# A top-1 mixture of experts on one core: the count of left-over tokens in eight portions over the third expert, its registers loaded and a GpSimd DRAIN placed earlier

## The chip, the cores and the metric

One Trainium2 chip, one of its cores. The metric is the device time of one execution in microseconds, lower is better. Engines are named as in the profile: PE is TensorE, DVE is VectorE, ACT is ScalarE, POOL is GpSimd, SP is SyncE, PEld the weight loads of TensorE. A name with a q behind it (POOLq) is the engine's sequencer, the queue that hands instructions to it.

## The reference, cut to what matters

```python
def _attn_ref(q, k, v):                       # 8 batches, 8 heads, 576 positions, 64 wide
    scores = np.matmul(q, k.transpose(0, 1, 3, 2)) / np.sqrt(64)
    return np.matmul(scores * Dmat[None], v)  # Dmat: a decay per head, causal
def _moe_ref(x, w_skip, w_gate, w1, w2):      # x: 4608 tokens x 512; 8 experts, 1024 hidden
    do_compute = x @ w_skip > 0
    out = x.copy()
    xc = x[do_compute]
    e_idx = np.argmax(xc @ w_gate, axis=1)
    gate_w = softmax(xc @ w_gate)[np.arange(len(xc)), e_idx]
    for e in range(8):
        mask = e_idx == e
        y[mask] = gate_w[mask, None] * (np.maximum(xc[mask] @ w1[e], 0.0) @ w2[e])
    out[do_compute] = xc + y
    return out
```

## The kernel before, in words

The first part, up to about 165 us, computes the retention for 36 tiles of 128 tokens, writes the tiles to `out`, and finds for each token its expert, its gate and its rank among the tokens of that expert.

The second part (`experts`, L1104) takes the experts one after the other, in an order found at run time from the largest to the smallest. Each expert has a fixed capacity (`CAPS`: 368, 344, 332, 308, 304, 286, 278, 276). Its tokens are gathered from `out` with three indirect DMAs on GpSimd (`gather_next`, L1059), turned, and split in a high and a low part (`xhi`, `xlo`). There are eight chunks of the hidden size. For a chunk, the up products write `ph`, ScalarE makes `hhi` from it and VectorE `hlo` (`rectify`, L521), and the down products read both and add to `py`. TensorE takes the up products of a chunk ahead of the down products of the chunk before it. After the eighth chunk `py` goes to `yT`, is turned back to token rows (`yn`), VectorE multiplies by the gate and adds the token (`rs`, L1040), and GpSimd scatters the rows to `out` with three indirect DMAs (`put_rows`, L1043). These scatters stand in the next expert, except for those of the first and the last expert. Weights come by SP in chunks of 512 KB; ScalarE makes `whi_w` and VectorE `wlo_w` (L164, L165), about five chunks ahead.

Tokens above a capacity are left over. `count_more` (L952) finds how many blocks of 128 of them there are: a small matmul `pn`, then VectorE instructions for `over`, `big`, `ends`, `sh`, the number `nmore`, and a new rank `trank` for the left-over tokens. It is called once, after the down products issued in chunk five of the last expert:

```python
        at(NE - 1, 4, 1, count_more)
...
    nblock = nc.values_load(nmore[0:1, 0:1], min_val=0, max_val=MAXB + NE)
    with tc.For_i(0, nblock, 1):
```

`at(e, f, place, do)` queues work into expert `e` (from 0), chunk `f` (from 0): place 0 ahead of the down products issued in that chunk, place 1 behind them. `values_load` (L1240) loads the number into a register of each of the five engines. The loop on it (L1241) does the left-over blocks; for these inputs it runs no time, and the kernel goes to its closing barrier (L1339).

TensorE's order is the order of the code (`manual_schedule`). On the other engines a scheduler sets it, guided by `keep_in_program_order`; `vec` (L176) is a VectorE instruction marked so, while `nc.vector...` alone is not. Where an instruction stands is therefore read from the built program, below.

Of the kernel before, what the change touches and what calls it, by code (L numbers as in the profile page):

```python
# [17 lines left out]
ALU = mybir.AluOpType  # L18
AX = mybir.AxisListType
# [3 lines left out]
NTOK, DM, NE, DF = B * S, H * D, 8, 1024  # L23
P = 128
# [5 lines left out]
NFC = DF // P  # L30
# [6 lines left out]
MAXB = -(-NTOK // P)  # L37
# [4 lines left out]
FAR = 1.0e5  # L42
# [23 lines left out]
def kernel(  # L66
# [9 lines left out]
    nc = tc.nc  # L76
# [10 lines left out]
    def bank(tag, name):  # L87

        if tag == "ph":
            tag = f"sc{turn[0] % 2}"  # L90
            turn[0] += 1
        return pm.tile([P, 512], F32, tag=TAGS.get(tag, tag), name=name)
# [16 lines left out]
    trank = const.tile([P, NT], F32, tag="trank", name="trank")  # L109
# [28 lines left out]
    mks = const.tile([P, NT, NE], BF16, tag="mks", name="mks")  # L138
    perm = const.tile([P, NE, NE], F32, tag="perm", name="perm")
    bump = const.tile([P, NE], BF16, tag="bump", name="bump")  # L140
    cape = const.tile([P, NE], F32, tag="cape", name="cape")
# [34 lines left out]
    def vec(name, *args, **kw):  # L176
        ins = getattr(nc.vector, name)(*args, **kw)  # L177
        if pinned[0]:
            tc.keep_in_program_order(ins)
        return ins  # L180
# [309 lines left out]
    nmore = const.tile([P, 1], I32, tag="nmore", name="nmore")  # L490
# [63 lines left out]
    with ExitStack() as actx:  # L554
# [224 lines left out]
        def logits_b(b, lt):  # L779
            pn = bank("lg", f"pn_{b}").rearrange("p (t i) -> p t i", i=P)  # L780
            for o in range(NB):
                nc.tensor.transpose(pn[:, o, :], lt[:, o * P : (o + 1) * P], ident)
            return pn
# [93 lines left out]
        for g in range(NT):  # L877
# [13 lines left out]
            if pn is not None:  # L891
                closed(g // NB - 1, pn)
                pn = None
# [12 lines left out]
            if lt is not None:  # L906
                pn = logits_b(g // NB - 1, lt)
# [19 lines left out]
        pn = logits_b(NT // NB - 1, lt)  # L927
# [18 lines left out]
    xr, xq, xts = {}, {}, {}  # L946

    xg0.append(mp.tile([P, DM], F32, tag="xg0_2", name="xg0_2", bufs=1))
    ends = rt.tile([P, NE], F32, tag="ends", name="ends")
    block = rt.tile([P, 1], F32, tag="block", name="block")  # L950

    def count_more():  # L952

        pn = bank("m", "pn")[:, :NE]
        nc.tensor.matmul(pn, ones, cum[:, len(GROUPS), :], start=True, stop=True)
        over = rt.tile([P, NE], F32, tag="over", name="over")
        nc.vector.tensor_tensor(over, pn, bump, ALU.add)
        nc.vector.tensor_tensor(over, over, cape, ALU.subtract)
        kb = [P, NE, MAXB]
        step = mp.tile([P, MAXB], F32, tag="step", name="step", bufs=1)  # L960
        nc.gpsimd.iota(step, pattern=[[P, MAXB]], base=0, channel_multiplier=0, allow_small_or_imprecise_dtypes=True)
        big = mp.tile(kb, F32, tag="big", name="big", bufs=1)
        nc.vector.tensor_tensor(
            big, over.unsqueeze(2).broadcast_to(kb), step.unsqueeze(1).broadcast_to(kb), ALU.is_gt
        )
        nc.vector.tensor_reduce(ends, big, axis=AX.X, op=ALU.add)

        sh = rt.tile([P, NE], F32, tag="sh", name="sh")
        nc.vector.memset(sh[:, 0:1], 0.0)
        for e in range(1, NE):  # L970
            nc.vector.tensor_copy(sh[:, e : e + 1], ends[:, e - 1 : e])
            nc.vector.tensor_tensor(ends[:, e : e + 1], ends[:, e : e + 1], ends[:, e - 1 : e], ALU.add)
        nc.vector.scalar_tensor_tensor(sh, sh, float(P), cape, ALU.mult, ALU.subtract)
        nc.vector.tensor_copy(nmore, ends[:, NE - 1 : NE])
        nc.vector.memset(block, 0.0)
        cb = [P, NT, NE]
        ct = mp.tile(cb, F32, tag="ct", name="ct", bufs=1)
        sums = []
        for n, x in (("cs", sh), ("cl", cape)):
            nc.vector.tensor_tensor(ct, mks, x.unsqueeze(1).broadcast_to(cb), ALU.mult)  # L980
            sums.append(mp.tile([P, NT], F32, tag=n, name=n, bufs=1))
            nc.vector.tensor_reduce(sums[-1], ct, axis=AX.X, op=ALU.add)
        cs, cl = sums
        nc.vector.tensor_tensor(cl, trank, cl, ALU.is_lt)
        nc.vector.tensor_tensor(trank, trank, cs, ALU.add)
        nc.vector.scalar_tensor_tensor(trank, cl, -FAR, trank, ALU.mult, ALU.add)

    def gather(e, xg, ks):
        for k, n in ks:
# [114 lines left out]
    def experts():  # L1104
# [20 lines left out]
        def at(e, f, place, do, *args):  # L1125
            between.setdefault((e, f, place), []).append(lambda: do(*args))
# [13 lines left out]
        def turn_next(e):  # L1140
# [3 lines left out]
            for c, where in enumerate([(4, 0), (5, 0), (5, 1), (6, 0), (7, 0)]):  # L1144
                if c:
                    at(e - 1, *where, split_turned, e, *xT[e], c - 1)
                if c < NCC:
                    at(e - 1, *where, turn_quarters, e, c)

        at(NE - 1, 4, 1, count_more)  # L1150
        for e in range(2, NE):
            at(e - 2, 4 if e > 2 else NCUT, 1, lambda e=e: gather_next(e, xg))

# [16 lines left out]
        for cur in steps + [None]:  # L1170
            if cur:
                e, f, ks = cur
# [15 lines left out]
            if last:  # L1188
                e, f, ks = last
# [44 lines left out]
    rectify(phs[5], early, hs[0, 5])  # L1234

    experts()
    mctx.__exit__(None, None, None)


    nblock = nc.values_load(nmore[0:1, 0:1], min_val=0, max_val=MAXB + NE)  # L1240
    with tc.For_i(0, nblock, 1):  # L1241
        puts.clear()
        mine = rt.tile([P, NE], F32, tag="mine", name="mine")
# [101 lines left out]
```

## Time and profile before

| | us |
|---|---|
| median of 3 runs | 412.4 (414.35, 406.65, 412.4) |
| the profiled execution | 408.29 |
| its span, first to last instruction | 406.6 |
| TensorE busy | 382.8 (94%) |
| VectorE busy | 260.3 (64%) |
| ScalarE busy | 150.5 (37%) |
| GpSimd busy | 126.5 (31%) |
| the last expert's chunks on TensorE | about 367 to 394 |
| the last row of any compute engine ends | 399.2 |

The span is 1.7 us shorter than the execution's own time. In the timeline a row is the start, the duration, the engine, the line, the operation, its output and inputs, and in brackets how long the engine was idle before it and who ended that. Matmuls overlap: the step from one start to the next is what one costs.

### The profile page before, as it was taken

The page shows a single profiled execution, that of the slowest core. Times are in us where ns is not written, and L with a number is a line of the kernel's source. Part 1 is how long each engine was busy: PE and PEld are TensorE (multiplying, and loading weights), DVE is VectorE, ACT ScalarE, POOL GpSimd, SP SyncE. Part 2 cuts the span into 40 slices and gives each one's busy share as a digit, 9 for nine tenths or more (in the row PEclk, how much of TensorE's full clock was granted, in tenths as well). Part 3 has the DMA queues.
Part 4 walks back from the last instruction along what each step waited for, and adds up shares of the span by engine and source line. Part 5 has one row for each costly group of instructions (what it writes and reads, how often), then busy time and mean ns, then how long its engine had stood idle before and what let it go on. Part 6 is the DMA issues. An engine that isn't in the chain of part 4 may idle for free. (4 is left out here: it accounts for less than half of the span.)

```text
span 406.6 us, 11777 instructions
## 1 busy us (share of the span) xinstructions
PE 382.8 (94%) x4840; PEld 346.4 (85%) x4840; DVE 260.3 (64%) x568; ACT 150.5 (37%) x264; POOL 126.5 (31%) x167
## 2 busy tenths in 40 slices
PE   8989999998999999999999999999999999999970
PEld 4768878777677778888999999999999999999970
DVE  3656775694496946758738566658567767677740
ACT  1222322332333345135435435526536355354110
POOL 5523232242363584260420032133230430402102
PEclk9999999999999999999999999999999999999995
DMA  8999998999999553083896596696786788844001
GB/s 302 408 394 312 389 374 261 358 332 379 389 340 374 188 182 106 24 282 119 266 272 220 194 278 196 200 273 205 214 292 204 228 273 248 254 150 131 23 2 55
DMA packets 38600, 98.50 MB, mean 242 GB/s; under 512 B 4523, under 2 KB 12075, under 8 KB 38544
## 3 DMA queue, kind: packets, MB, share of 16 engines
q1 hardware_dynamic: 29584, 78.13, 57.6%
q0 software_dynamic: 3488, 10.03, 7.3%
q10 hardware_dynamic: 5472, 9.56, 6.3%
q8 instruction: 39, 0.64, 0.7%
q14 instruction: 17, 0.14, 0.1%
HBM read 79.72 MB, written 18.35 MB: 241 GB/s over the span
## 5 line engine op out<-in xcount | busy, mean ns | idle before, releaser
L164 ACT CAST whi_w<-w 128x1024 fp32r<-128x1024 f32 x58 | 60.9, 1051 | 47.9 <-DMA w<-w 25.1
L1044 POOL DMA_INDIRECT out<-rs,sidx x24 | 34.1, 1422 | 135.1 <-DVE rs L1040 134.1
L165 DVE TENSOR_TENSOR wlo_w<-w,whi_w 128x1024 fp32r<-128x1024 f32 x58 | 69.8, 1204 | 0.0
L503 PE MATMUL py<-hlo,whi_w 128*128 128x344 f32 (+6 forms) x224 | 67.9, 303 | 1.7 <-DVE hlo L527 1.6
L503 PE MATMUL ph<-xhi,whi_w 128*128 128x344 f32 (+6 forms) x224 | 68.8, 307 | 0.0
L503 PE MATMUL py<-hhi,whi_w 128*128 128x344 f32 (+6 forms) x224 | 68.2, 305 | 0.0
L503 PE MATMUL ph<-xlo,whi_w 128*128 128x344 f32 (+6 forms) x224 | 67.7, 302 | 0.3 <-DVE xlo L172 0.3
L503 PE MATMUL py<-hhi,wlo_w 128*128 128x344 f32 (+6 forms) x224 | 67.7, 302 | 0.0
L503 PE MATMUL ph<-xhi,wlo_w 128*128 128x344 f32 (+6 forms) x224 | 67.7, 302 | 0.0
L671 POOL TENSOR_TENSOR v<-v,tt_sb 128x512 f32<-128x512 f32 x36 | 37.5, 1043 | 82.7 <-DVE xt L177 59.3
L527 DVE SCALAR_TENSOR_TENSOR hlo<-ph,hhi 128x344 fp32r<-128x344 f32 (+7 forms) x58 | 27.4, 474 | 40.3 <-ACT hhi L526 39.8
L761 ACT COPY xn<-px 128x512 f32<-128x512 f32 x36 | 21.1, 586 | 85.1 <-PE px L759 77.2
L177 DVE TENSOR_TENSOR sc<-psc,mask 128x512 f32<-128x512 f32 x72 | 46.2, 683 | 9.8 <-PE psc L636 5.1
L177 DVE TENSOR_TENSOR xt<-pxt,gt_sb 128x256 f32<-128x256 f32 x72 | 27.0, 416 | 39.0 <-PE pxt L729 36.4
L526 ACT ACTIVATE hhi<-ph 128x344 fp32r<-128x344 f32 (+7 forms) x58 | 24.7, 426 | 62.5 <-PE ph L503 58.8
L503 PEld LDWEIGHTS py<-hlo,whi_w 128*128 128x128 f32 x224 | 42.2, 188 | 2.1 <-DVE hlo L527 2.1
L503 PEld LDWEIGHTS ph<-xlo,whi_w 128*128 128x128 f32 x224 | 42.3, 189 | 0.6 <-DVE xlo L172 0.5
L503 PEld LDWEIGHTS ph<-xhi,whi_w 128*128 128x128 f32 x224 | 42.2, 188 | 0.2
L503 PEld LDWEIGHTS py<-hhi,whi_w 128*128 128x128 f32 x224 | 42.2, 188 | 0.0
L503 PEld LDWEIGHTS py<-hhi,wlo_w 128*128 128x128 f32 x224 | 42.2, 188 | 0.0
L503 PEld LDWEIGHTS ph<-xhi,wlo_w 128*128 128x128 f32 x224 | 42.2, 188 | 0.0
L708 PE MATMUL pxt<-sc,v 128*64 128x128 f32 x576 | 39.9, 275 | 0.0
(194 smaller groups left out, 595.2 us busy)
## 6 DMA issues: line engine op xcount, KB each, us to landing
w<-w SPq DMA_DIRECT2D x64, 512.0 KB
q<-qkv SPq DMA_DIRECT2D x36, 512.0 KB
v<-qkv SPq DMA_DIRECT2D x32, 512.0 KB
out<-xn ACTq DMA_DIRECT2D x36, 256.0 KB
xr<-xg SPq DMA_DIRECT2D x6, 512.0 KB
xq<-xr SPq DMA_DIRECT2D x12, 144.0 KB
xq<-xr SPq DMA_DIRECT2D x8, 160.0 KB
v<-qkv SPq DMA_DIRECT2D x4, 256.0 KB
```

The lines of the kernel that those rows point to most:

```text
L164: nc.scalar.copy(hi, t)
L165: ins = nc.vector.tensor_tensor(lo, t, hi.bitcast(F32), ALU.subtract)
L177: ins = getattr(nc.vector, name)(*args, **kw)
L503: nc.tensor.matmul(ps, x, y, start=first and n == 0, stop=last and n == 3 * len(terms) - 1)
L526: nc.scalar.activation(hi, ph, AF.Relu)
L527: keep(nc.vector.scalar_tensor_tensor(lo, ph, 0.0, hi.bitcast(F32), ALU.max, ALU.subtract))
L671: ins = nc.gpsimd.tensor_tensor(v, v, vt_sb[:, place(g), :].unsqueeze(2).broadcast_to([P, H, D]), ALU.mult)
L708: nc.tensor.matmul(pxt[a % 2][halves[j], a // 2, :], v[:, head(a, r), :], sc[:, r, a, :], start=a < 2, stop=t == 0 and a >= NPR - 2, skip_ ...
L761: nc.scalar.copy(xn, px)
L1044: put = nc.gpsimd.indirect_dma_start(out=out, out_offset=bass.IndirectOffsetOnAxis(ap=sidx[:n, k, e : e + 1], axis=0), in_=rs[:n], in_offs ...
```

## The change

`count_more` becomes a generator whose eight portions stand in the eight chunks of the third expert (e = 2), behind the down products of each. Its VectorE instructions are kept in order. `load_count` holds the loads of the number into the five engines' registers; it and a DRAIN of GpSimd are called in chunk four of the last expert, behind the down products.

```diff
+    nblock = None
...
-        nc.vector.tensor_tensor(over, pn, bump, ALU.add)
-        nc.vector.tensor_tensor(over, over, cape, ALU.subtract)
+        vec("tensor_tensor", over, pn, bump, ALU.add)
+        vec("tensor_tensor", over, over, cape, ALU.subtract)
...
+        yield
+        vec("tensor_tensor", big, over.unsqueeze(2).broadcast_to(kb), step.unsqueeze(1).broadcast_to(kb), ALU.is_gt)
+        vec("tensor_reduce", ends, big, axis=AX.X, op=ALU.add)
+        yield
...
         for e in range(1, NE):
-            nc.vector.tensor_copy(sh[:, e : e + 1], ends[:, e - 1 : e])
-            nc.vector.tensor_tensor(ends[:, e : e + 1], ends[:, e : e + 1], ends[:, e - 1 : e], ALU.add)
+            vec("tensor_copy", sh[:, e : e + 1], ends[:, e - 1 : e])
+            vec("tensor_tensor", ends[:, e : e + 1], ends[:, e : e + 1], ends[:, e - 1 : e], ALU.add)
+            if e % 3 == 0:
+                yield
+        vec("scalar_tensor_tensor", sh, sh, float(P), cape, ALU.mult, ALU.subtract)
+        vec("tensor_copy", nmore, ends[:, NE - 1 : NE])
+        vec("memset", block, 0.0)
+        yield
...
         for n, x in (("cs", sh), ("cl", cape)):
+            vec("tensor_tensor", ct, mks, x.unsqueeze(1).broadcast_to(cb), ALU.mult)
             sums.append(mp.tile([P, NT], F32, tag=n, name=n, bufs=1))
+            vec("tensor_reduce", sums[-1], ct, axis=AX.X, op=ALU.add)
+            yield
...
+    def load_count():
+
+        nonlocal nblock
+        nblock = nc.values_load(nmore[0:1, 0:1], min_val=0, max_val=MAXB + NE)
...
-        at(NE - 1, 4, 1, count_more)
+        portions = count_more()
+        for f in range(NFC):
+            at(2, f, 1, next, portions, None)
+        at(NE - 1, 3, 1, load_count)
+        at(NE - 1, 3, 1, lambda: tc.keep_in_program_order(nc.gpsimd.drain()))
...
-    nblock = nc.values_load(nmore[0:1, 0:1], min_val=0, max_val=MAXB + NE)
     with tc.For_i(0, nblock, 1):
```

What the scheduler makes of it, at three places. First GpSimd in the third expert. `xg_4` and `xg_5` are the gathers for the fifth and sixth expert (counted from 0), `rs_2` the scatters of the third. Before:

```order
L411 DMA xg_4_3958<-out,gidx_133 128x512 x2
L411 DMA xg_4_3958<-out,gidx_133 64x512
L1044 DMA out<-rs_2_0_4176,sidx_134 4608x512
L1044 DMA out<-rs_2_1_4214,sidx_134 4608x512
L1044 DMA out<-rs_2_2_4236,sidx_134 4608x512
L411 DMA xg_5_4313<-out,gidx_133 128x512 x2
L411 DMA xg_5_4313<-out,gidx_133 32x512
```

And now, on GpSimd at the same place:

```order
L411 DMA xg_4_3987<-out,gidx_133 128x512 x2
L411 DMA xg_4_3987<-out,gidx_133 64x512
L995 TENSOR_LOAD nmore_137
L1053 DMA out<-rs_2_0_4215,sidx_134 4608x512
L1053 DMA out<-rs_2_1_4253,sidx_134 4608x512
L1053 DMA out<-rs_2_2_4275,sidx_134 4608x512
L411 DMA xg_5_4352<-out,gidx_133 128x512 x2
L411 DMA xg_5_4352<-out,gidx_133 32x512
```

GpSimd's load of the number, which was the last row ahead of the loop, now stands in the third expert. This listing leaves DRAINs out; in the built program the new DRAIN is the instruction right behind this TENSOR_LOAD, so it stands in the third expert too, although the code calls it in the last.

Second, VectorE in chunks five to seven of the third expert (`hlo_2_4` to `hlo_2_6`). Before:

```order
L527 SCALAR_TENSOR_TENSOR hlo_2_4_3929<-ph_2_4_0_3927,hhi_2_4_3928 128x332
L1093 STREAM_TRANSPOSE xt_3_0_3944<-xq_3_3849 128x320
L165 TENSOR_TENSOR wlo_w_3_0_3781_3969<-w_3_0_3781,whi_w_3_0_3781_3968 128x1024
L527 SCALAR_TENSOR_TENSOR hlo_2_5_3976<-ph_2_5_0_3974,hhi_2_5_3975 128x332
L172 TENSOR_TENSOR xlo_3_3756<-xt_3_0_3944,xhi_3_3755 128x320
L1093 STREAM_TRANSPOSE xt_3_1_3993<-xq_3_3849 128x320
L172 TENSOR_TENSOR xlo_3_3756<-xt_3_1_3993,xhi_3_3755 128x320
```

And now, on VectorE from the transpose behind `hlo_2_4` on:

```order
L1102 STREAM_TRANSPOSE xt_3_0_3968<-xq_3_3859 128x320
L177 COPY sh_3886<-ends_2979 128x1
L177 TENSOR_TENSOR ends_2979<-ends_2979 128x1
L177 SCALAR_TENSOR_TENSOR sh_3886<-sh_3886,cape_126 128x8
L177 CAST nmore_137<-ends_2979 128x1
L177 MEMSET block_2980 128x1
L165 TENSOR_TENSOR wlo_w_3_0_3789_3998<-w_3_0_3789,whi_w_3_0_3789_3997 128x1024
L527 SCALAR_TENSOR_TENSOR hlo_2_5_4005<-ph_2_5_0_4003,hhi_2_5_4004 128x332
L172 TENSOR_TENSOR xlo_3_3756<-xt_3_0_3968,xhi_3_3755 128x320
L1102 STREAM_TRANSPOSE xt_3_1_4022<-xq_3_3859 128x320
L177 TENSOR_TENSOR ct_4036<-mks_123,sh_3886 128x288
L177 TENSOR_REDUCE cs_4038<-ct_4036 128x36
```

Portion five, with the number itself, and portion six stand between the weights, `hlo` and the next expert's tokens.

Third, VectorE in the last expert, from the split of weight chunk seven on. Before:

```order
L165 TENSOR_TENSOR wlo_w_7_6_5464_5638<-w_7_6_5464,whi_w_7_6_5464_5637 128x1024
L527 SCALAR_TENSOR_TENSOR hlo_7_3_5643<-ph_7_3_0_5641,hhi_7_3_5642 128x276
L165 TENSOR_TENSOR wlo_w_7_7_5501_5671<-w_7_7_5501,whi_w_7_7_5501_5670 128x1024
L527 SCALAR_TENSOR_TENSOR hlo_7_4_5676<-ph_7_4_0_5674,hhi_7_4_5675 128x276
L957 TENSOR_TENSOR over_5705<-pn_5703,bump_125 128x8
L958 TENSOR_TENSOR over_5705<-over_5705,cape_126 128x8
L963 TENSOR_TENSOR big_5710<-over_5705,step_5708 128x288
```

And now, on VectorE from the same split on:

```order
L165 TENSOR_TENSOR wlo_w_7_6_5503_5677<-w_7_6_5503,whi_w_7_6_5503_5676 128x1024
L995 TENSOR_LOAD nmore_137
L165 TENSOR_TENSOR wlo_w_7_7_5540_5725<-w_7_7_5540,whi_w_7_7_5540_5724 128x1024
L527 SCALAR_TENSOR_TENSOR hlo_7_3_5682<-ph_7_3_0_5680,hhi_7_3_5681 128x276
L527 SCALAR_TENSOR_TENSOR hlo_7_4_5730<-ph_7_4_0_5728,hhi_7_4_5729 128x276
L527 SCALAR_TENSOR_TENSOR hlo_7_5_5759<-ph_7_5_0_5757,hhi_7_5_5758 128x276
```

The count is gone from here, `hlo_7_5` follows `hlo_7_4`, VectorE's load of the number has come in, and `hlo_7_3` stands behind the last weight split. On TensorE the load stands between the down products of chunk three and the up products of chunk five of the last expert, on SP in the third expert ahead of weight chunk five of the fourth, and on ScalarE at the end as before.

## Rows read from the trace of the kernel before

**Rows 1.** The page: span, and busy time of each engine.
```profile
span 406.6 us, 11777 instructions
PE 382.8 (94%) x4840; PEld 346.4 (85%) x4840; DVE 260.3 (64%) x568; ACT 150.5 (37%) x264; POOL 126.5 (31%) x167
```

**Rows 2.** Waits from 380 to 400: us in total, times, longest.
```profile
PE py L503 <- DVE hlo L527: 1.6, 1, 1.6
```

**Rows 3.** Timeline of TensorE in the last expert.
```profile
379.42 0.29 PE L503 MATMUL py<-hhi,whi_w 128*128 128x276 f32 x1
379.54 0.29 PE L503 MATMUL py<-hlo,whi_w 128*128 128x276 f32 x1
...
380.94 0.18 PE L955 MATMUL pn<-cum,ones 128*128 128x8 bf16 x1
...
385.63 0.29 PE L503 MATMUL py<-hhi,whi_w 128*128 128x276 f32 x1
387.56 0.39 PE L503 MATMUL py<-hlo,whi_w 128*128 128x276 f32 x1 [1.64 <-DVE hlo L527]
```

**Rows 4.** Timeline of VectorE in the last expert; first and last of the count.
```profile
375.71 1.20 DVE L165 TENSOR_TENSOR wlo_w<-w,whi_w 128x1024 fp32r<-128x1024 f32 x1
377.01 0.45 DVE L527 SCALAR_TENSOR_TENSOR hlo<-ph,hhi 128x276 fp32r<-128x276 f32 x1
377.37 1.21 DVE L165 TENSOR_TENSOR wlo_w<-w,whi_w 128x1024 fp32r<-128x1024 f32 x1
...
381.17 0.17 DVE L957 TENSOR_TENSOR over<-pn,bump 128x8 f32<-128x8 f32 x1 [0.68 <-PE pn L955]
...
386.95 0.20 DVE L986 SCALAR_TENSOR_TENSOR trank<-cl,trank 128x36 f32<-128x36 f32 x1
387.07 0.79 DVE L527 SCALAR_TENSOR_TENSOR hlo<-ph,hhi 128x276 fp32r<-128x276 f32 x2
```

**Rows 5.** Busy time by stretch: the third expert; columns in the first line.
```profile
core 0: us, PE busy (x) PEld busy (x) DVE busy (x) ACT busy (x) POOL busy (x), PEclk, DMA share, GB/s
225.30:254.60 29.30, 29.30 (x196) 29.23 (x196) 18.59 (x29) 13.10 (x22) 7.48 (x6) 1.00 0.72 228
```

**Rows 6.** Timeline of VectorE in the third expert, `hlo` of chunks seven and eight.
```profile
249.81 0.49 DVE L527 SCALAR_TENSOR_TENSOR hlo<-ph,hhi 128x332 fp32r<-128x332 f32 x1
...
253.37 0.50 DVE L527 SCALAR_TENSOR_TENSOR hlo<-ph,hhi 128x332 fp32r<-128x332 f32 x1 [1.14 <-ACT hhi L526]
```

**Rows 7.** Timeline of TensorE there: the first readers of these two.
```profile
252.79 0.31 PE L503 MATMUL py<-hlo,whi_w 128*128 128x332 f32 x1
...
256.32 0.31 PE L503 MATMUL py<-hlo,whi_w 128*128 128x332 f32 x1
```

**Rows 8.** Timeline of GpSimd: last gather for the fifth expert, and scatters.
```profile
247.12 0.94 POOL L411 DMA_INDIRECT xg<-out,gidx  x1 [0.30 <-issue]
263.05 1.77 POOL L1044 DMA_INDIRECT out<-rs,sidx  x1 [14.99 <-DVE rs L1040]
...
398.32 0.90 POOL L1044 DMA_INDIRECT out<-rs,sidx  x1 [0.30 <-issue]
```

**Rows 9.** Instructions of L1339 and L1336: ns least/median/most, first and last start.
```profile
L1339 SPq DRAIN  x3: 7/7/7, 401.2 to 406.0; - x3
L1339 POOLq DRAIN  x3: 51/103/3984, 401.8 to 406.3; - x3
...
L1336 POOLq DRAIN  x1: 197/197/197, 0.4 to 0.4; - x1
```

**Rows 10.** Waits of SP's queue from 380 on: total, times, longest.
```profile
SPq L1241 <- DMA out<-rs,sidx: 14.2, 3, 13.3
```

**Rows 11.** Instructions of L1240, as in rows 9.
```profile
L1240 PEldq TENSOR_LOAD <-nmore x1: 483/483/483, 394.4 to 394.4; - x1
L1240 DVEq TENSOR_LOAD <-nmore x1: 542/542/542, 395.6 to 395.6; - x1
```

**Rows 12.** Timeline of TensorE's weight loads at the end.
```profile
394.33 0.92 PEld L1038 LDWEIGHTS yn<-ident,yT 128*128 128x128 f32 x9 [0.30 <-DVE yT L1023]
```

More of the change, by code (lines that the diff above doesn't have):

```diff
@@ L962, in count_more @@
         big = mp.tile(kb, F32, tag="big", name="big", bufs=1)
[L963 to L966, printed above, removed]
+        yield
+        vec("tensor_tensor", big, over.unsqueeze(2).broadcast_to(kb), step.unsqueeze(1).broadcast_to(kb), ALU.is_gt)
+        vec("tensor_reduce", ends, big, axis=AX.X, op=ALU.add)
+        yield
         sh = rt.tile([P, NE], F32, tag="sh", name="sh")
-        nc.vector.memset(sh[:, 0:1], 0.0)
+        vec("memset", sh[:, 0:1], 0.0)
         for e in range(1, NE):
-            nc.vector.tensor_copy(sh[:, e : e + 1], ends[:, e - 1 : e])
-            nc.vector.tensor_tensor(ends[:, e : e + 1], ends[:, e : e + 1], ends[:, e - 1 : e], ALU.add)
-        nc.vector.scalar_tensor_tensor(sh, sh, float(P), cape, ALU.mult, ALU.subtract)
-        nc.vector.tensor_copy(nmore, ends[:, NE - 1 : NE])
-        nc.vector.memset(block, 0.0)
+            vec("tensor_copy", sh[:, e : e + 1], ends[:, e - 1 : e])
[6 more added lines that the diff above has]
+        yield
         cb = [P, NT, NE]
@@ L979, in count_more @@
         for n, x in (("cs", sh), ("cl", cape)):
-            nc.vector.tensor_tensor(ct, mks, x.unsqueeze(1).broadcast_to(cb), ALU.mult)
+            vec("tensor_tensor", ct, mks, x.unsqueeze(1).broadcast_to(cb), ALU.mult)
             sums.append(mp.tile([P, NT], F32, tag=n, name=n, bufs=1))
-            nc.vector.tensor_reduce(sums[-1], ct, axis=AX.X, op=ALU.add)
+            vec("tensor_reduce", sums[-1], ct, axis=AX.X, op=ALU.add)
+            yield
         cs, cl = sums
-        nc.vector.tensor_tensor(cl, trank, cl, ALU.is_lt)
-        nc.vector.tensor_tensor(trank, trank, cs, ALU.add)
-        nc.vector.scalar_tensor_tensor(trank, cl, -FAR, trank, ALU.mult, ALU.add)
+        vec("tensor_tensor", cl, trank, cl, ALU.is_lt)
+        vec("tensor_tensor", trank, trank, cs, ALU.add)
+        vec("scalar_tensor_tensor", trank, cl, -FAR, trank, ALU.mult, ALU.add)
+    def load_count():
+        nonlocal nblock
+        nblock = nc.values_load(nmore[0:1, 0:1], min_val=0, max_val=MAXB + NE)
     def gather(e, xg, ks):
```

## The prediction

> **What bounds the kernel now.** I read the page first. TensorE is busy for 382.8 of 406.6 us [rows 1], so whatever is to be won is either a hole in TensorE's work or the part of the span in which TensorE has nothing left. The waits of the last 26 us show one hole of size, 1.6 us in `py` behind VectorE's `hlo` [rows 2]. TensorE's timeline gives its place: matmuls of the last expert follow each other 0.12 to 0.13 us apart (379.42, 379.54), but after 385.63 the next starts at 387.56 [rows 3]. VectorE's timeline gives its cause: from 381.17 to 387.07 the 27 instructions of the count run back to back, and the `hlo` that TensorE wants stands behind them [rows 4]. Third, the tail. GpSimd ends its last scatter at 398.32 + 0.90 = 399.22 [rows 8]. SyncE waits 13.3 us for the scatters to land [rows 10], and the engines come to the closing barrier from 401.2 on. There GpSimd's first DRAIN takes 3984 ns from 401.8, while the two after it take 51 and 103 ns and the one at the program's start 197 ns [rows 9]. So 3.98 of the last 4.8 us are one DRAIN, and no engine computes beside it.
>
> **The change part by part.**
>
> The count leaves the last expert. Without it TensorE's step from 385.63 should be the usual 0.13 us in place of 1.93: **1.80 us** off the path. What is late next? `hlo` of the sixth chunk needs only ScalarE's `hhi` of that chunk, and VectorE is idle at the time; its chunk four lands before 377.50 and is wanted at 379.54 [rows 3, 4], so this wait has some 2 us in hand everywhere else. The path behind it (last down products, `yT`, transposes, `rs`, three scatters, landing) keeps its lengths and moves forward with TensorE. The small matmul `pn` (0.18 us, at 380.94) only moves to the third expert, where it costs TensorE what it cost here.
>
> The count enters the third expert. Its 5.9 us of VectorE (381.17 to 387.07) now stand in eight pieces there. VectorE is busy for 18.6 of that expert's 29.3 us [rows 5], so 5.9 more make 24.5, which fits, if no piece comes between a `hlo` and TensorE in time. The last pieces come where VectorE is fullest. Piece six is a product and a reduction of 0.46 + 0.45, about 0.95 us with the gap. I follow the stream on from it: chunk seven's `hlo` (249.81 before) slips to about 250.2, piece seven adds 0.95, and chunk eight's `hlo` (253.37) slips to about 253.6 [rows 6]. TensorE wants them at 252.79 and 256.32 [rows 7], and they took 0.50 us: more than 2 us in hand for each. Cost 0. If the cover were gone, the whole 5.9 us could become TensorE waits; a gain is excluded, since nothing leaves this expert. The weight loads wait for VectorE's `wlo`, which slips by at most a piece; the chunks are split about five ahead (some 18 us of products), so nothing of that reaches TensorE.
>
> The register loads. Five engines load the count with one TENSOR_LOAD each. VectorE's took 542 ns at the end and TensorE's 483 [rows 11]. TensorE's began at 394.4, with nine weight loads following from 394.33 on for 0.92 us [rows 12]: the sequencer's load lay beside queued work. I therefore take 0 for TensorE's load, now in front of the fifth up product, with 0.48 us as the other end. VectorE's load now stands behind `wlo` of chunk seven, and `hlo` of chunk four now behind `wlo` of chunk eight. In the old times: `wlo` ends at 376.91, the next takes 1.21, and `hlo` is done at about 378.5, or 379.1 with the load fully exposed, against 379.54. Cost 0, other end 0.5. SyncE's load has the number before it needs it, since the same VectorE queue frees its next buffer only after `nmore` is written. ScalarE's stays at its end. GpSimd's leaves the tail, but the last scatter there is paced by the scatter before it, so I take 0, with half a us as the bound of a gain.
>
> The DRAIN. The order shows GpSimd's TENSOR_LOAD in the third expert, behind the gather for the fifth and ahead of the third's scatters; the DRAIN is the next instruction of that stream, not, as the code reads, in the last expert. Behind it are queued the scatters, and behind these the next gather. GpSimd ends the gather at 247.12 + 0.94 = 248.06 and starts the first scatter at 263.05 [rows 8]: 15 us free. The DRAIN there costs between 0.05 and 3.98 us [rows 9], so it is hidden at either end. It would have to last over 14 us to delay a scatter.
>
> What it does to the closing DRAIN is the open term. Each expert has three gathers and three scatters, 48 in all; 21 stand ahead of the new DRAIN and 27 behind it. The page has only two kinds: 3.98 us after 48 of them, and 0.05 to 0.20 us with none of them since the last DRAIN [rows 9]. So a DRAIN clears something. If that grows with each DMA it is 83 ns of each, and 27 leave 2.24 us: **1.74 us** off. If it is there at full size after any such DMA, nothing goes; if only the first DRAIN pays, some 3.9 us go. The rows lie between the ends: 27 is nearer to 48 than to none, which is what the share by count says, and I take that.
>
> Here the Trainium skill speaks against the change. The page "PSUM — Partial Sum Buffer", section "Engine vs sequencer instructions", says a drain waits for the engine to go fully idle, so an earlier one leaves nothing behind and the last waits only for what still runs. The trace agrees only in part: it shows no GpSimd work after 399.22, yet 3.98 us of DRAIN from 401.8. By that rule the new DRAIN would save nothing, which is the first rival below.
>
> **The sum.** The profiled execution took 408.29 us, with a span of 406.6. 1.80 + 1.74 = 3.5 us off, so 404.8 on its scale. That execution is the second shortest of the four times shown (414.35, 412.40, 408.29, 406.65), which have a mean of 410.4; the median of three is 412.4. I put the forecast on the mean of the four: 410.4 - 3.5 = **406.9 us**.
>
> **The rivals**, on the same scale:
> - The closing DRAIN stays at 3.98 us: only TensorE's hole goes. 410.4 - 1.8 = 408.6. For it: one DRAIN of size is all there is to read, and 27 DMAs follow the new one. Against it: the short DRAINs right behind the long one.
> - The new DRAIN takes nearly all of it, the closing one being short: 410.4 - 1.8 - 3.9 = 404.7. Against it: new scatters follow.
> - VectorE becomes the bound of the third expert, and the answer is slower. Its place is the `hlo` of chunks seven and eight behind pieces six and seven; it decides from the point at which they slip by over 2.4 us, and its price is at most the 5.9 us of the count: 410.4 - 1.8 + 5.9 = 414.5. For it: the two largest pieces fall where the next expert's tokens are split too. Against it: the slip worked out is 0.4.
> - The change does not do what it says: the hole in the last expert remains, filled by TensorE's register load or by `hlo` behind `wlo`, and the DRAIN is as before. 410.4.
>
> **How the numbers follow.** Chances: share by count 0.42, DRAIN unchanged 0.34, DRAIN nearly gone 0.11, VectorE bound 0.06, no effect 0.07. The times shown of the same kernel lie 3.8 us below and 3.9 us above their mean, so a median carries some 3 us of its own. The range goes from the nearly-gone case less 2.5, about 402, to the unchanged case and 4 more, about 412.5. A measurement of this kernel can tell about 2% from no change, some 8 us, and no case reaches that by itself. Faster by over 2% needs the best case with a low draw: 0.07. Slower by over 2% needs the slower rival with a high draw: 0.03. The rest, 0.90, is within 2%.
>
> **What would show it.** Right: in the last expert no wait of `py` for `hlo` over 0.2 us, and VectorE idle between `hlo`s from 380 to 390; in the third expert no new TensorE wait; on GpSimd a DRAIN between 248 and 253 that is followed by idle time, and a closing DRAIN of about 2.2 us. A closing DRAIN near 4 us says the size does not come from the count of DMAs; one below 0.5 us says that the first one pays for all. Wrong: TensorE waits behind `hlo` at 249 to 257, a hole at TensorE's register load in the last expert, or scatters of the third expert that start later than `rs` is ready.

## The result, and the profile after

The changed kernel took 403.63 us (median of four runs, 403.48 to 405.4), the kernel before 410.24 us (median of four, 406.65 to 414.35). The ratio is 0.9883 with a 95% interval of 0.9834 to 0.9932. Ratios, here and below, are of fast runs alone and are not quotients of the medians beside them: among the runs below, one of 409.51 us of the version with the DRAIN alone is slow and left out of its ratio. So the change is about 1.2% faster, clear of the noise but within the 2% that count as the same. The forecast was 406.9 us, range 402.0 to 412.5, "within 2%" at 0.90.

The profiled execution took 403.77 us with a span of 402.1 us, 4.5 us shorter than the one before (406.6). To see where they went I used the transposes `yn`, which turn an expert's result back to token rows: their first row is a mark at the same place of the program in every run. (Except for the last expert, they stand early in the next one.) These are the marks of the second, the third, the seventh and the last expert in TensorE's timeline of the kernel before:

```profile
231.21 0.60 PE L1038 MATMUL yn<-ident,yT 128*128 128x128 f32 x4
...
261.38 0.60 PE L1038 MATMUL yn<-ident,yT 128*128 128x128 f32 x4
...
370.45 0.60 PE L1038 MATMUL yn<-ident,yT 128*128 128x128 f32 x4
...
393.63 1.90 PE L1038 MATMUL yn<-ident,yT 128*128 128x128 f32 x12
```

The same marks in TensorE's timeline of the changed kernel:

```profile
230.49 0.60 PE L1047 MATMUL yn<-ident,yT 128*128 128x128 f32 x4
...
260.64 0.60 PE L1047 MATMUL yn<-ident,yT 128*128 128x128 f32 x4
...
369.71 0.60 PE L1047 MATMUL yn<-ident,yT 128*128 128x128 f32 x4
...
390.85 1.90 PE L1047 MATMUL yn<-ident,yT 128*128 128x128 f32 x12
```

| stretch | before | after | difference |
|---|---|---|---|
| start to the first mark | 231.21 | 230.49 | -0.72 |
| first to second mark: the third expert | 30.17 | 30.15 | -0.02 |
| second to third mark: four experts | 109.07 | 109.07 | 0.00 |
| third to fourth mark: the last expert | 23.18 | 21.14 | -2.04 |
| fourth mark to GpSimd's closing DRAIN | 8.17 | 8.15 | -0.02 |
| that DRAIN to the end of the span | 4.8 | 3.1 | -1.7 |

Two stretches carry the gain, and they are the two of the prediction: the last expert, and the closing DRAIN. The first 0.72 us are no part of it. The nine other profiled runs below reach the first mark anywhere between 229.74 and 234.01, versions with and without the portions mixed, so such a difference is one between executions.

Only the first portion lies ahead of the first mark: `pn`, at 226.70, takes TensorE 0.27 us from its start to the second next matmul in place of 0.15. That is the 0.12 us that it cost in the last expert before, so it moved without gain or loss.

**The last expert.** VectorE's timeline there, in the changed kernel, answers to [rows 4]:

```profile
374.97 2.34 DVE L165 TENSOR_TENSOR wlo_w<-w,whi_w 128x1024 fp32r<-128x1024 f32 x2
377.24 0.43 DVE L527 SCALAR_TENSOR_TENSOR hlo<-ph,hhi 128x276 fp32r<-128x276 f32 x1
379.32 0.45 DVE L527 SCALAR_TENSOR_TENSOR hlo<-ph,hhi 128x276 fp32r<-128x276 f32 x1 [1.65 <-ACT hhi L526]
382.36 0.45 DVE L527 SCALAR_TENSOR_TENSOR hlo<-ph,hhi 128x276 fp32r<-128x276 f32 x1 [2.59 <-ACT hhi L526]
385.40 0.45 DVE L527 SCALAR_TENSOR_TENSOR hlo<-ph,hhi 128x276 fp32r<-128x276 f32 x1 [2.60 <-ACT hhi L526]
```

From 379.32 on every `hlo` waits only for ScalarE, and the brackets show VectorE idle for 1.6 to 2.6 us ahead of each. TensorE's timeline at the matmul that had the hole answers to the last two of [rows 3]:

```profile
384.77 0.29 PE L503 MATMUL py<-hhi,whi_w 128*128 128x276 f32 x1
384.90 0.29 PE L503 MATMUL py<-hlo,whi_w 128*128 128x276 f32 x1
385.02 0.29 PE L503 MATMUL py<-hhi,wlo_w 128*128 128x276 f32 x1
```

The step from the first to the second is 0.13 us, where it was 1.93.

**The third expert.** Busy time by stretch, the 29.30 us that answer to [rows 5]:

```profile
core 0: us, PE busy (x) PEld busy (x) DVE busy (x) ACT busy (x) POOL busy (x), PEclk, DMA share, GB/s
224.58:253.88 29.30, 29.30 (x197) 29.10 (x196) 22.37 (x55) 13.02 (x22) 7.49 (x6) 1.00 0.70 216
```

TensorE is busy for the whole stretch, as before, at a granted clock of 1.00, the 2.4 GHz level. VectorE's timeline around the two largest portions answers to [rows 6]:

```profile
246.54 0.42 DVE L177 TENSOR_TENSOR ct<-mks,sh 128x288 f32<-128x288 bf16 x1
246.99 0.45 DVE L177 TENSOR_REDUCE cs<-ct 128x36 f32<-128x288 f32 x1
...
249.86 0.49 DVE L527 SCALAR_TENSOR_TENSOR hlo<-ph,hhi 128x332 fp32r<-128x332 f32 x1
...
253.05 0.50 DVE L527 SCALAR_TENSOR_TENSOR hlo<-ph,hhi 128x332 fp32r<-128x332 f32 x1
```

And their first readers in TensorE's timeline, which answer to [rows 7]:

```profile
252.06 0.31 PE L503 MATMUL py<-hlo,whi_w 128*128 128x332 f32 x1
...
255.59 0.31 PE L503 MATMUL py<-hlo,whi_w 128*128 128x332 f32 x1
```

Chunk seven's `hlo` ends at 249.86 + 0.49 = 250.35 and is wanted at 252.06: 1.71 us in hand, 2.49 before. Chunk eight's has 2.04 in hand, 2.45 before. The portions made them later by 0.78 and 0.41 us against TensorE, and nothing reached TensorE.

**GpSimd and the end.** The DRAINs and register loads of the changed kernel (columns as in [rows 9]; L1163 is the new DRAIN, L995 the loads):

```profile
L1163 POOLq DRAIN  x1: 5873/5873/5873, 245.8 to 245.8; - x1
...
L1351 SPq DRAIN  x3: 7/7/7, 398.4 to 401.5; - x3
L1351 POOLq DRAIN  x3: 51/103/2257, 399.0 to 401.8; - x3
...
L995 POOLq TENSOR_LOAD <-nmore x1: 500/500/500, 245.2 to 245.2; - x1
L995 DVEq TENSOR_LOAD <-nmore x1: 545/545/545, 374.3 to 374.3; - x1
L995 PEldq TENSOR_LOAD <-nmore x1: 732/732/732, 374.9 to 374.9; - x1
```

GpSimd's timeline around the new DRAIN, which answers to [rows 8]:

```profile
246.96 0.94 POOL L411 DMA_INDIRECT xg<-out,gidx  x1 [0.30 <-issue]
262.31 1.77 POOL L1053 DMA_INDIRECT out<-rs,sidx  x1 [14.41 <-DVE rs L1049]
```

The new DRAIN ends at about 251.6 (245.75 + 5.87), over 10 us ahead of the first scatter, whose idle time ends with VectorE's `rs` as before. The closing DRAIN takes 2257 ns, not 3984. TensorE's load began at 374.9, 2.2 us ahead of the matmuls that follow it in program order (the fifth up products, from 377.16, one step of 0.12 us behind the last down product). The sequencer runs that far ahead of the engine, and its 732 ns cost nothing.

### The profile page after: what moved, and what is told of

It reads as the page before. It is cut to its first block, busy times and chain, and to the rows that moved or that the text cites. A ratio compares the mean times of both kernels' runs of the same rounds, so it can differ in the third digit from the quotient of the medians.

```text
span 402.1 us, 11778 instructions
## 1 busy us (share of the span) xinstructions
PE 381.8 (95%) x4840; PEld 345.7 (86%) x4840; DVE 259.8 (65%) x568; ACT 150.5 (37%) x264; POOL 129.1 (32%) x167
## 5 line engine op out<-in xcount | busy, mean ns | idle before, releaser
L1053 POOL DMA_INDIRECT out<-rs,sidx x24 | 35.3, 1469 | 129.1 <-DVE rs L1049 127.2
```

The source lines that it names most:

```text
L1053: put = nc.gpsimd.indirect_dma_start(out=out, out_offset=bass.IndirectOffsetOnAxis(ap=sidx[:n, k, e : e + 1], axis=0), in_=rs[:n], in_offs ...
```

## The experiments

Two theories stood against each other for each half. For the last expert: the hole is VectorE's count and nothing else, or part of it comes back elsewhere. For the end: the closing DRAIN goes by the number of indirect DMAs that GpSimd issued since its last DRAIN (83 ns each), or by their rows, or by the time since then. Edits are to the changed kernel unless the text says otherwise.

### The count in portions alone, without the DRAIN

```diff
-        at(NE - 1, 3, 1, lambda: tc.keep_in_program_order(nc.gpsimd.drain()))
```

> The changed kernel without its new DRAIN, so all else of the change alone. Theory of two separate gains (the hole in the last expert, and a closing DRAIN that takes 83 ns for each indirect DMA since the DRAIN before it): 48 DMAs, so the closing DRAIN is back at 3.98 us; no wait of py for hlo over 0.2 us in the last expert; about 2.0 us less than before, a ratio near 0.995. Rival, the moved count or register load shortens the closing DRAIN: it stays near 2.26 us and the ratio is near 0.991.

Measured: 406.35 us (ten runs) against 407.88 (thirteen) for the kernel before, ratio 0.9975 (0.9944 to 1.0007). Its last expert takes 390.12 - 368.98 = 21.14 us, so the hole is gone. The time alone would not show it, since the interval takes in 1. Its closing barrier reads:

```profile
L1350 POOLq DRAIN  x3: 51/103/3984, 398.2 to 402.8; - x3
```

That is the 3984 ns of the kernel before to the nanosecond. The portions and the moved loads give the last expert's part, and they leave the closing DRAIN as it was.

### The DRAIN alone, in the kernel before, behind the seventh expert's scatters

```diff
+        at(NE - 1, 3, 1, lambda: tc.keep_in_program_order(nc.gpsimd.drain()))
         at(NE - 1, 4, 1, count_more)
```

> The kernel before with one DRAIN of GpSimd added behind the scatters of the seventh expert, 45 of the 48 indirect DMAs ahead of it; the count stays in the last expert. Closing DRAIN by count of DMAs: 3 x 83 ns = 0.25 us. By rows moved since the last DRAIN (0.79 ns each, 276 rows): 0.22 us. By time since the last DRAIN (the two runs give 1.26 us + 6.8 ns for each us): 1.4 us. The hole of 1.6 us stays in the last expert. By count or rows about 3.7 us less than before, ratio near 0.991; by time 2.6 us less.

Measured: 403.89 us (four runs) against 407.88, ratio 0.9892 (0.9846 to 0.9938). The count stays in the last expert and so does the hole. The waits from 376 on have it, and the last expert takes 393.40 - 370.24 = 23.16 us:

```profile
PE py L503 <- DVE hlo L527: 1.6, 1, 1.6
```

But with only three scatters behind the new DRAIN the closing barrier reads:

```profile
L1340 POOLq DRAIN  x3: 51/103/297, 401.5 to 402.4; - x3
```

Three DMAs at 82 ns, and the 51 ns of a DRAIN that follows another with no DMA between, make 297. The new DRAIN ended some 20 us before (375.6 + 5.6), a twentieth of the span, so neither a length in proportion to the time since then nor the 1.4 us of the line through two runs fits. The profiled execution also loses 1.0 us that the others don't, in the four experts ahead of the last (370.24 - 260.17 = 110.07, elsewhere 109.07 to 109.10), before its new DRAIN begins; its span, 402.6 us, says that much too little for the DRAIN.

### The DRAIN late, and the count in portions

```diff
-        at(NE - 1, 3, 1, load_count)
         at(NE - 1, 3, 1, lambda: tc.keep_in_program_order(nc.gpsimd.drain()))
+        at(NE - 1, 3, 1, load_count)
```

This swaps two lines. With the load called first, GpSimd's TENSOR_LOAD and the DRAIN behind it both stand in the third expert. With the DRAIN first it stands behind the seventh expert's scatters, and the load among the last ones (395.2). My reading is that the kept order pins an instruction only behind the one of its engine that was written before it, and that nothing held the load in the last expert. How the scheduler chose was not followed: in the version without the new DRAIN the same load stays in the last expert (393.3).

> The changed kernel with the two calls swapped, so that the DRAIN stands where the code calls it, behind the scatters of the seventh expert, with three indirect DMAs behind it. The two gains add: closing DRAIN 0.25 us, no hole; 2.0 + 3.7 = 5.7 us less than before, ratio near 0.986, and some 2.0 us less than the changed kernel. Rival, the DRAIN there holds the last scatters up: it starts near 378, clears 45 DMAs in 3.7 us and ends by 383, against a first scatter at 393, so only one of over 14 us would.

Measured: 402.76 us against 407.88, ratio 0.987 (0.9831 to 0.9909), span 401.3. Last expert 392.04 - 370.90 = 21.14 us.

```profile
L1351 POOLq DRAIN  x3: 51/103/297, 400.2 to 401.0; - x3
```

The ratios of the two halves, run apart above, multiply to it: 0.9975 × 0.9892 = 0.9867. Within their intervals the gains add.

### All eight portions at once, in chunk five of the third expert

```diff
-            at(2, f, 1, next, portions, None)
+            at(2, 4, 1, next, portions, None)
```

> The changed kernel with all eight portions in one place, chunk five of the third expert. VectorE then has 5.9 us of count between hlo of chunk five and hlo of chunk six. Theory that the cutting is what hides it: hlo of chunk six slips from about 245.3 to 250 and TensorE, which wants it near 248.4, waits 1.5 to 2.5 us there, so the gain in the last expert is given back. Rival, any place in the third expert is as good: no wait over 0.3 us.

Measured (one run): 406.47 us, span 404.8. TensorE's timeline, behind VectorE's count from 243.22 to 249.25:

```profile
250.85 0.42 PE L503 MATMUL py<-hlo,whi_w 128*128 128x332 f32 x1 [1.96 <-DVE hlo L527]
```

VectorE's timeline ahead of it: the count's last instruction, then a weight split, and only then the `hlo` of chunk six:

```profile
249.05 0.20 DVE L177 SCALAR_TENSOR_TENSOR trank<-cl,trank 128x36 f32<-128x36 f32 x1
249.16 1.22 DVE L165 TENSOR_TENSOR wlo_w<-w,whi_w 128x1024 fp32r<-128x1024 f32 x1
250.30 0.50 DVE L527 SCALAR_TENSOR_TENSOR hlo<-ph,hhi 128x332 fp32r<-128x332 f32 x1
```

The third expert takes 263.34 - 230.69 = 32.65 us, 2.5 more than in every version with the portions spread, and the last one 393.55 - 372.42 = 21.13. So the hole only moves when the count stays in one piece: TensorE has about 2.5 us in hand over `hlo`, and 6 us of VectorE in a row used it up in both experts where they stood. This is the slower rival's mechanism in its place, and what the spreading is for.

### The DRAIN behind the fifth expert's scatters

```diff
+        at(5, 3, 1, lambda: tc.keep_in_program_order(nc.gpsimd.drain()))
         at(NE - 1, 3, 1, load_count)
-        at(NE - 1, 3, 1, lambda: tc.keep_in_program_order(nc.gpsimd.drain()))
```

> The changed kernel with its DRAIN behind the scatters of the fifth expert, 36 indirect DMAs ahead of it and 12 behind it. The closing DRAINs so far fit 0.05 us + 82 ns for each DMA since the DRAIN before it. By that count 12 leave 1.03 us. By rows moved (1128 rows at 0.79 ns) 0.89 us. By time since the last DRAIN (some 75 us, at 1.26 us + 6.8 ns for each us) 1.8 us.

Measured (one run): 403.62 us, span 401.9. Twelve DMAs stand behind the DRAIN here, and 51 + 12 × 82 = 1035:

```profile
L1351 POOLq DRAIN  x3: 51/103/1033, 400.1 to 401.6; - x3
```

The new DRAIN itself is the longest seen, and this time something is queued behind it, the gathers for the eighth expert:

```profile
L1162 POOLq DRAIN  x1: 8289/8289/8289, 323.5 to 323.5; - x1
```

It ends at 331.8, the gather starts at 332.78, 7.4 us after the last scatter ended. With no DRAIN there this gap is 5.5 us in the kernel before and 5.4 to 6.8 in the other versions, so the gather is later by 0.7 to 2 us. TensorE's marks show nothing of it (four experts 370.78 - 261.68 = 109.10, last expert 391.91 - 370.78 = 21.13): the gather was early enough.

### Scatters of few rows

This version's scatters of the third to the seventh expert write only the first 16 rows of each tile; the other rows of these experts don't reach the output. The number of DMAs is the same.

```diff
-            put_rows(e, k, n, rs)
+            put_rows(e, k, min(n, 16) if e in range(2, 7) else n, rs)
```

> The changed kernel, but the scatters of the third to seventh expert write only their first 16 rows, so those tokens' results are left out of the output. The number of indirect DMAs is the same, 27 behind the DRAIN; the rows behind it fall from 2648 to 1380. By count of DMAs the closing DRAIN stays at 2.26 us; by rows it falls to 1.1 us.

Measured (one run): 407.37 us. This execution reached the first mark at 234.01, before any of the shortened scatters, so some 3 us of it have nothing to do with the edit. The DRAIN has its old length to the nanosecond:

```profile
L1351 POOLq DRAIN  x3: 51/103/2257, 402.5 to 405.3; - x3
```

Rows, and so bytes, don't set it. The number of DMAs does, as the counts of 3, 12 and 48 show beside it.

### The register loads back at the end

To the version with the late DRAIN; the loads go back to just ahead of the loop.

```diff
-        at(NE - 1, 3, 1, load_count)
...
+    load_count()
     with tc.For_i(0, nblock, 1):
```

> The version with the DRAIN behind the seventh expert's scatters, with the call that loads the left-over count into the engines' registers put back to its place just ahead of the loop, as in the kernel before; the portions of the count and the DRAIN stay. If moving the loads is worth nothing (my theory: TensorE's sequencer is some 2 us ahead of its matmuls when it loads), the last expert's layer-normalisation transposes follow those of the seventh expert by 21.1 us again, the closing DRAIN takes 297 ns, and the span is that of the version with the loads early, within 1 us apart from what stands before the third expert. If the loads held TensorE back in their old place, the last expert takes 0.5 to 1 us longer. If it is the early loads that cost time, the stretch from the start of the last expert to the end is shorter by 0.3 us or more.

Measured (one run): 403.81 us, span 402.1. The last expert takes 392.80 - 371.67 = 21.13 us. From its start to the end of the span are 402.1 - 371.67 = 30.43 us; in the version with early loads (profiled again, below) 400.6 - 370.19 = 30.41.

```profile
L995 PEldq TENSOR_LOAD <-nmore x1: 484/484/484, 393.6 to 393.6; - x1
L995 POOLq TENSOR_LOAD <-nmore x1: 508/508/508, 396.0 to 396.0; - x1
```

Moving the loads is worth nothing either way.

### The changed kernel and the late DRAIN side by side

Both unchanged: the changed kernel, and the version with the two lines swapped.

> The changed kernel as it is, timed on one chip beside the version with the late DRAIN. Both terms of the sum stand: ratio near 0.99 of before, about 3.8 us less.

> The changed kernel with the DRAIN behind the seventh expert's scatters, timed again on the same chip. By count its closing DRAIN is 24 x 82 ns = 2.0 us shorter than that of the changed kernel, so it is 2.0 us faster than that, ratio near 0.986 of before. Rival, something else gives the 2 us back: the two have the same time.

Measured on one chip, with the kernel before at 408.77 us (fourteen runs): the changed kernel 404.79 (nine runs), ratio 0.9905 (0.9873 to 0.9937); the late DRAIN 402.59 (six runs), ratio 0.9854 (0.9818 to 0.989). The closing DRAINs are 2257 and 297 ns again. By the DRAIN alone the second should be 1.96 us shorter than the first; the medians are 2.2 apart. The late DRAIN is the fastest version of this study.

## Why the prediction was right

**The hole in the last expert: mechanism right, a little under-sized.** The prediction had 1.80 us, the step of 1.93 less a usual one. The last expert lost 2.04 us. The rest is in two steps that it left out: the matmul behind the hole needed 0.23 us to the next (387.56 to 387.79) in place of 0.13, and `pn` 0.25 us from 380.94 to the second next matmul in place of 0.13. That is 1.80 + 0.10 + 0.12 = 2.02. The last 0.12 is only moved to the start of the third expert (`pn` at 226.70), so the net is about 1.9.

**The closing DRAIN: right, and for the reason given.** The share by count said 2.24 us left and 1.74 off; it is 2.257 and 1.73. Four counts now lie on one line:

| indirect DMAs since the DRAIN before | 3 | 12 | 27 | 48 |
|---|---|---|---|---|
| closing DRAIN, ns | 297 | 1033 | 2257 | 3984 |
| 51 + 82 × count | 297 | 1035 | 2265 | 3987 |

So the choice "nearer to 48 than to none" came out, but its ground was weak: two points, 48 and none, can't tell a line from a step. The rival with the DRAIN unchanged had 0.34 for that reason, and it fell on the first row of the trace.

**A rule that spoke against it.** GpSimd's last row ends at 395.55 + 0.90 = 396.45 and the closing DRAIN starts 2.55 us later, as before (2.58); from there it takes 0.3 to 4.0 us by the number of DMAs issued long ago. The rule of the Trainium skill (page "PSUM — Partial Sum Buffer", section "Engine vs sequencer instructions") that a drain waits until the engine is wholly idle, read as a wait for what still runs, would have given the same length in every version. The measurement decides against that reading. A DRAIN in the middle does wait for what still runs, as the last section shows, but the price by the number of DMAs comes on top.

**The third expert: right that it costs nothing, but the slips are twice what it had.** The `hlo` of chunks seven and eight slip by 0.78 and 0.41 us, where the prediction followed the stream to 0.4 and 0.2. VectorE's busy time there rose to 22.37 us, not 24.5: the 5.9 us were elapsed time with its gaps, and the portions' 27 instructions are busy for 4.68 us of the stretch, which has one weight split fewer in it. Both errors lie far inside the 2.5 us in hand. The version with the count in one piece shows where they would not have: 1.96 us of wait.

**The new DRAIN: hidden as forecast, bound wrong.** Its place and the free time behind it were read correctly, and the cover of 15 us held. The bound of 3.98 us counted only the DMAs and had no term for gathers that have not landed yet. The row lasts 5.87 us, of which some 2.1 lie ahead of the end of the last gather's row (247.90); from there it took 3.73 us, inside the bound, but 4.43 when the same kernel was profiled again. In the version behind the fifth expert's scatters it took 6.40 and stayed hidden for another reason, the slack of a gather.

**The register loads: right at 0.** The last expert is 21.13 us with them inside it and 21.13 with them behind it.

**The sum.** Predicted 3.5 us off. The parts in the trace make 2.04 + 1.73 - 0.12 = 3.65. On a base of 410.24 that is a ratio of 0.9911, inside both measured intervals (0.9834 to 0.9932, and 0.9873 to 0.9937). The medians of the first comparison lie 6.6 us apart and the first ratio, 0.9883, gives 4.8 us; both are more than the trace holds, and the runs of the kernel before in that comparison spread over 7.7 us. So what the first comparison shows beyond 3.65 is luck between executions; in the second, of 14 and nine runs, the medians lie 4.0 apart. The forecast of 406.9 was 3.3 us above the median mostly because of its base: it put the kernel before at 410.4, and 13 and 14 later runs of it have medians of 407.88 and 408.77.

## What to carry to other kernels

When no engine computes at the end of a program, read the closing barrier row by row: on this chip GpSimd's DRAIN took 82 ns for each indirect DMA that GpSimd had issued since its last DRAIN, and another DRAIN in an idle stretch behind most of them takes that off the end (3.98 us down to 0.30). Put it as late as its idle stretch allows, with room for the DMAs ahead of it to land, and look in the built order where it came to stand: with a register load called just ahead of it, it stood five experts earlier than with the two lines swapped. Serial small work on a helper engine is free only in pieces smaller than the lead which that engine has over the one that bounds: 6 us in one piece cost 2.0 to 2.5 us in either expert, eight pieces of under 1 us nothing.

## What the runs showed of the hardware that was not expected

The closing DRAIN repeats to the nanosecond at a given count (3984 in two kernels, 2257 in four profiled runs, 297 in four), whatever rows the DMAs moved. All DMAs have landed by then: in the changed kernel the last one at 397.64, the DRAIN starts at 399.0.

A DRAIN placed in the middle can be longer than that count gives. From the end of the last DMA's row to its own end it took 3.75 us in the four profiled runs that have it late, behind 45 DMAs (51 + 45 × 82 = 3741 ns), so there the count explains it. Behind 21 DMAs, in the third expert, it took between 2.9 and 4.4 us, where the count gives 1.77; behind 36 DMAs, in the sixth expert, 6.4, where the count gives 3.0.

The traces also have the time at which each DMA landed, and this tells what the rest is: the DRAIN waits for the last landing.

| version | DMAs ahead | last DMA's row ends | last landing | DRAIN ends | landing to end |
|---|---|---|---|---|---|
| count in one piece | 21 | 247.89 | 249.89 | 250.80 | 0.91 |
| changed kernel | 21 | 247.90 | 250.72 | 251.63 | 0.91 |
| scatters of few rows | 21 | 251.37 | 254.30 | 255.20 | 0.91 |
| changed kernel, profiled again | 21 | 248.90 | 252.43 | 253.33 | 0.91 |
| behind the fifth expert | 36 | 325.35 | 330.24 | 331.76 | 1.52 |
| late DRAIN | 45 | 379.28 | 380.54 | 383.03 | 2.49 |

The landing comes 2.0 to 3.5 us after the row's end in the first four, and the DRAIN's end follows it by the same 0.91 us each time. That is half of the count's price (51 + 21 × 41 = 912 ns); for 36 DMAs half is 1527 ns. In the late place the last landing comes 1.3 us after the row's end in all four runs, before half of the price (1.9 us) is over, and nothing is waited for. So all nine ends fit one reading to 0.02 us: half of the price runs from the end of the last DMA's row, then the DRAIN waits for the last landing, then the other half runs. The fixed distance to the landing is in the rows; the two halves are only a fit, made after the runs, and no run was set up to try it. VectorE's work beside the DRAIN does not explain the lengths: with the count in one piece VectorE is busy for 2.77 of the 2.91 us, and that DRAIN is the shortest of the four behind 21 DMAs.

Whoever hides a DRAIN should leave it room for the DMAs ahead of it to land, and not only the length that the closing one shows.

The load of one number into a register took 271 to 276 ns on SyncE, 462 to 464 on ScalarE, 500 to 511 on GpSimd, 541 to 545 on VectorE and on TensorE 483 or 484 at the end and 725 to 737 inside the last expert (543 in the version with scatters of few rows).
